# Two small softmax products with 64 stationary columns instead of twice 32

## The chip, the core and the metric

The kernel runs on one core of one Trainium2 chip. A core has a matrix engine (TensorE, PE in the profile; its weight loads are listed apart as PEld), VectorE (DVE), ScalarE (ACT) and GpSimd (POOL), and a SyncE (SP) that issues the DMA transfers here. The metric is the device time of one execution in microseconds, the median of the runs shown.

## The reference

A Fourier filter over the sequence, and then a mixture of experts with soft routing over all tokens of all batches:

```
X = np.fft.rfft(x, axis=1)                 # x: 8 batches, 2496 tokens, 256 channels
y = np.fft.irfft(X * (filt_r + 1j * filt_i), n=2496, axis=1)
x = y.reshape(8 * 2496, 256)
logits = x @ phi                           # 32 slots: 8 experts with 4 each
d = softmax of logits over the 19968 tokens    (dispatch)
slot_input = d.T @ x
slot_out = relu(slot_input @ w1[e]) @ w2[e]    (per expert, 256 -> 1024 -> 256)
c = softmax of logits over the 32 slots        (combine)
out = c @ slot_out
```

## The kernel before

The transform of 2496 points is split into 39 by 64. A first stage (`s1_unit`, L312 to L327, and `first_unit` for batch 0) multiplies by the 39-point matrix and puts the result through DRAM in another order; `x_unit` (L343) multiplies by the 64-point matrix C("b") and, on DVE and POOL, with the filter; `t_unit` (L369) transposes the filtered spectrum into the tiles `y`, and multiplies it by phi into the logits' spectrum `lts`. The inverse transform of the full 256 channels is never made: softmax needs only the logits in the token domain, which have 32 columns per batch, and the slot input is summed in the spectral domain.

The main loop (L734) has a slot for each pair of spectral columns, ten to a batch, and in each slot runs an x unit, the first-stage units that fall due, and a t unit two slots behind. When a pair of batches is through (GROUPS, four pairs), `chain(g)` (L409) is started for it, a generator that `hop` advances by one or more steps per slot, so that its work lies among the units. The last group's chain runs after the loop, with the held rest of the group before in its gaps (`behind`, L403), and then the experts (`h` at L859, `o` at L876) and the output products (L912).

A chain's steps, in order, with what the change and the prediction touch:

- `lsb` (L432 to L441): each batch's logits' spectrum, 5 tiles of 4 columns t by 32 slots, is transposed and copied by DVE.
- `v1` (L442 to L458): the inverse first stage. For each of the 20 columns t the spectrum (128 rows, 32 slots of one batch) is the stationary operand and one half of the constant `minv` (66 columns) the moving one. Two batches and two halves h give four products for a t. Each writes 32 partitions of one PSUM tile, so each sits in its own strip of 32 columns of the matrix engine. Seven t's fill a PSUM tile, which ACT copies into SBUF.
- `v`, `lg` (L459 to L486): transposes and the 39-point product give the logits `lg` in the token domain, with the running maximum (`cm`, `cmax`, `mt`, `mb`, `m_new`).
- `dispatch` (L512): DVE subtracts the maximum, ACT takes the exponential: `d`.
- `u` (L520 to L544): the forward first stage of `d`. For each of the 22 row blocks a (two halves h of 11) `d` for one batch (117 rows, 32 slots) is stationary and one half th of `w1d` (60 columns) moves: again four products with 32 partitions each.
- `u2`, `dd` (L545 to L571): transposes and the 64-point product give the spectrum of the dispatch weights.
- `z`, `s` (L573 to L613): with `dd` as the stationary operand, the sum of the weights and the slot input are accumulated over the `y` tiles. After its last use a `y` tile is free; the expert weights (`load_ws`, L725) are loaded into such tiles.
- the combine weights (L616 to L636): maximum, exponential and reciprocal sum over the slots. For groups 0 and 1 `lg` is put out to DRAM (L639) and read back for the tail (L785).

PE's work stands in the program order of the tile scheduler, which places instructions with a timeline of its own (L975). PE takes its instructions in order; only weight loads are pulled ahead. A matrix product in 32-bit floats is two records, and so is its weight load.

Of the kernel before, what the change touches and what calls it, by code (L numbers as in the profile page):

```python
# [9 lines left out]
F32 = mybir.dt.float32  # L10
F32R = mybir.dt.float32r
AF = mybir.ActivationFunctionType
ALU = mybir.AluOpType
# [6 lines left out]
NT = 20  # L20
NI = 22
NH = 11
PK = 3
KR = PK * N1
# [11 lines left out]
SLOTS = NE * SPE  # L36
GROUPS = ((0, 1), (2, 3), (4, 5), (6, 7))
NG = len(GROUPS)
NSPILL = 2
OUT_ORDER = (4, 5, 0, 1, 2, 3, 6, 7)  # L40
P = 128
SCALE = 2.0 / SEQ
NM = BATCH * SQ // P
KP = N2 + 2
# [162 lines left out]
def fft_soft_moe(ctx, tc, x, fr, fi, phi, w1, w2, cst, w1q, out):  # L207
    nc = tc.nc
    pe, dve, act, pool_e, sp = nc.tensor, nc.vector, nc.scalar, nc.gpsimd, nc.sync

    const = ctx.enter_context(tc.tile_pool(name="const", bufs=1))
    scr = ctx.enter_context(tc.tile_pool(name="scr", bufs=3, space=DRAM))
# [14 lines left out]
    r_all = const.tile([KR, NG, 4 * NH], F32, name="r_all")  # L227
# [6 lines left out]
    def C(name, lo=0, hi=None):  # L234
        o, rows, cols = OFF[name]
        hi = cols if hi is None else hi
        return cst_t[0:rows, o + lo : o + hi]
# [7 lines left out]
    lgp_cm, lgp = open_pool("lgp", 1, "left")  # L245
# [151 lines left out]
    c_dram = {}  # L397

    lgs = {}
# [9 lines left out]
    def chain(g):  # L409
        bs = GROUPS[g]  # L410
        wk = late_pool[0] if g == NG - 1 else work
# [4 lines left out]
        def copy(engine, dst, src):  # L416
            if g == NG - 1:
                engine = (dve, act)[flip[0] % 2]
                flip[0] += 1
            if engine is act:  # L420
                act.copy(dst, src)
            else:
                dve.tensor_copy(dst, src)
# [5 lines left out]

        nb = len(bs)  # L430
        R = nb * 64
        lsb = wk.tile([P, nb, NT, SLOTS], F32, tag="cc", name=f"lsb_{g}", bufs=1)  # L432
        for b2, b in enumerate(bs):
            lf = lsb[:, b2].rearrange("k t e -> k (t e)")
            for i0 in (0, 4):
                pl = psum([P, 4, P], f"ltr_{b}_{i0}")
                n = min(4, 5 - i0)
                for i in range(n):
                    pe.transpose(pl[:, i, :], lts[b][:, i0 + i, :], ident)
                copy(dve, lf[:, i0 * P : (i0 + n) * P], pl.rearrange("k i q -> k (i q)")[:, 0 : n * P])  # L440
            yield  # L441
        v1 = wk.tile([P, KP // 2, 2, NT], F32, tag="ca", name=f"v1_{g}", bufs=1)  # L442
        for t0 in range(0, NT, 7):
            n = min(7, NT - t0)
            pv = psum([P, 7, KP // 2, 2], f"v1_{g}_{t0}")
            for t in range(t0, t0 + n):
                for b2 in range(nb):
                    for h in range(2):
                        q = (b2 * 2 + h) * 32
                        pe.matmul(  # L450
                            pv[q : q + 32, t - t0].rearrange("q k r -> q (k r)"),
                            lsb[:, b2, t, :],
                            C("minv" if t else "minv0", h * KP, (h + 1) * KP),
                            start=True,
                            stop=True,
                        )
            copy(act, v1[0:R, :, :, t0 : t0 + n], pv[0:R, 0:n].rearrange("q t k r -> q k r t"))
            yield  # L458
        v = wk.tile([QP, NH, R], F32, tag="cb", name=f"v_{g}", bufs=1)  # L459
        lg_t = lgp.tile([KR, NH, nb, 2, SLOTS], F32, tag=f"lg{max(g, NSPILL)}", name=f"lg_{g}")  # L460
        lgs[g] = lg_t
        lg = lg_t.rearrange("s a b h e -> s a (b h e)")
        cm = wk.tile([KR, 3, SLOTS], F32, tag="cm", name=f"cm_{g}", bufs=1)
        v1f = v1.rearrange("q k r t -> q (k r t)")
        SA = 512 // R
        for s0 in range(0, NH, SA):
            n = min(SA, NH - s0)
            pv = psum([QP, SA, R], f"v_{g}_{s0}")
# [5 lines left out]
        for s0 in range(0, NH, SA):  # L474
            n = min(SA, NH - s0)
            pv = psum([KR, SA, R], f"lg_{g}_{s0}")
# [10 lines left out]
        nch = -(-NH // SA)  # L487

        NX = 2 * nb * NH
        lgf = lg_t.rearrange("s a b h e -> s (a b h) e")  # L490
        dve.tensor_reduce(out=cmax, in_=cm[:, 0:nch].rearrange("s c e -> s e c"), axis=AX.X, op=ALU.max)
        m_new, m_old = m_run[g], m_run[g - 1]
        pm = psum([SLOTS, KR], f"mt_{g}")
# [10 lines left out]
        else:  # L504
            dve.tensor_copy(m_new, pmb)
        d = wk.tile([KR, NX, SLOTS], F32, tag="cb", name=f"d_{g}", bufs=1)
        dv = d.rearrange("s (a b h) e -> s a b h e", b=nb, h=2)
        HT = NT // 2
        u = wk.tile([P, HT, 2 * N2], F32, tag="ca", name=f"u_{g}", bufs=1)
        mbc = m_new[0:KR].rearrange("s (o e) -> s o e", o=1)  # L510
# [9 lines left out]
        for a0 in range(0, NH, 4):  # L520
            n = min(4, NH - a0)
            if a0 + 4 < NH:
                dispatch(a0 + 4)
            pu = psum([P, 2, 4 * PK * 2, HT], f"u_{g}_{a0}")
            for h in range(2):
                for a in range(a0, a0 + n):
                    i = h * NH + a
                    kr, jn = (KR, PK) if i < NI - 1 else (N1, 1)
                    r0 = (a - a0) * 2 * PK
                    for b2 in range(nb):  # L530
                        for th in range(2):
                            q = (b2 * 2 + th) * 32
                            pe.matmul(
                                pu[q : q + 32, h, r0 : r0 + 2 * jn].rearrange("q r t -> q (r t)"),
                                dv[0:kr, a, b2, h, :],
                                C("w1d", th * PK * NT, th * PK * NT + jn * NT)[0:kr],
                                start=True,
                                stop=True,
                            )
            for h in range(2):  # L540
                k0 = (h * NH + a0) * PK * 2
                nk = min((h * NH + a0 + n) * PK, N2) * 2 - k0
                copy(act, u[0:R, :, k0 : k0 + nk], pu[0:R, h, 0:nk].rearrange("q r t -> q t r"))
            yield  # L544
        u2 = wk.tile([P, HT, nb, 2, SLOTS], F32, tag="cc", name=f"u2_{g}", bufs=1)  # L545
        for t0 in range(0, HT, SA):
            n = min(SA, HT - t0)
            pu = psum([P, SA, R], f"u2_{g}_{t0}")
            for t in range(n):
                pe.transpose(pu[:, t, :], u[0:R, t0 + t, :], ident[0:R, 0:R])  # L550
            copy(dve, u2[:, t0 : t0 + n].rearrange("k t b h e -> k t (b h e)"), pu[:, 0:n])
            if t0 != 0:
                yield
        dd = wk.tile([P, HT, nb, 2, SLOTS], F32, tag="cb", name=f"dd_{g}", bufs=1)
        for t0 in range(0, HT, SA):
            n = min(SA, HT - t0)
            pd = psum([P, SA, R], f"dd_{g}_{t0}")
            pe.matmul(
                pd[:, 0:n],
                C("b"),  # L560
                u2[:, t0 : t0 + n].rearrange("k t b h e -> k t (b h e)"),
                start=True,
                stop=True,
            )
            copy(act, dd[:, t0 : t0 + n].rearrange("k t b h e -> k t (b h e)"), pd[:, 0:n])
            if t0 == 0:
                dve.tensor_scalar(
                    out=dd[:, 0, :, 0, :], in0=dd[:, 0, :, 0, :], scalar1=C("wh"), scalar2=None, op0=ALU.mult
                )
            else:  # L570
                yield  # L571
# [4 lines left out]
        for b2 in range(nb):  # L576
            for j in range(4):
                pe.matmul(
                    pz[32 * j : 32 * j + 32, :], dd[:, 0, b2, 0, :], C("e0"), start=(b2 == 0), stop=(b2 == nb - 1)
                )  # L580
        if g > 0:
            al = wk.tile([P, SLOTS], F32, tag="al", name=f"al_{g}", bufs=1)
# [12 lines left out]
        for b2, b in enumerate(bs):  # L595
            for t in range(NT):
                j = t % 4
                with behind(g, b2 * NT + t):
                    pe.matmul(  # L599
                        pss[32 * j : 32 * j + 32, :],  # L600
                        dd[:, t % HT, b2, t // HT, :],
                        ys[b, t // 2][:, t % 2, :],
                        start=(b2 == 0 and t < 4),
                        stop=(b2 == nb - 1 and t >= NT - 4),
                    )
                if t % 8 == 7:
                    yield
# [27 lines left out]
        dve.tensor_scalar(out=rs, in0=rs, scalar1=1e-9, scalar2=None, op0=ALU.add)  # L635
        dve.reciprocal(out=rs, in_=rs)  # L636
        if g < NSPILL:
            c_dram[g] = scr.tile([KR, NH, nb, 2, SLOTS], F32, name=f"c_dram{g}", bufs=1)
            sp.dma_start(c_dram[g], lg_t)  # L639

    def load_tables(c):
# [139 lines left out]
    ltp_cm.__exit__(None, None, None)  # L781
    tail_cm, tail = open_pool("tail", 2, "left")
    for g in range(NSPILL):
        lgs[g] = tail.tile([KR, NH, len(GROUPS[g]), 2, SLOTS], F32, tag="cl", name=f"cl_{g}", bufs=NSPILL)
        sp.dma_start(lgs[g], c_dram[g])  # L785

    zr = const.tile([P, 1], F32, name="zr")
# [20 lines left out]
    def combine(pos):  # L808
# [4 lines left out]
        g, b2 = where[b]  # L813
        nb = len(GROUPS[g])
        cl = lgs[g]
        rv = r_all[:, g, 0 : 2 * nb * NH].rearrange("s (a b h) -> s a b h", b=nb, h=2)
        c1 = tail.tile([KR, 2, NH, SLOTS], F32, tag="c1", name=f"c1_{b}")
        for h in range(2):
            rb = rv[:, :, b2, h : h + 1].broadcast_to([KR, NH, SLOTS])
            nc.gpsimd.tensor_tensor(out=c1[:, h], in0=cl[:, :, b2, h], in1=rb, op=ALU.mult)  # L820
        cq = tail.tile([KR, 2, 4, SLOTS], F32, tag="cr", name=f"cr_{b}")
        nc.gpsimd.tensor_copy(cq[:, 0, 0:3], c1[:, 0, 8:11])
        nc.gpsimd.tensor_copy(cq[:, 0, 3:4], c1[:, 1, 8:9])
# [155 lines left out]
```

## Time and profile before

| | us |
|---|---|
| runs shown: median (lowest to highest) of 3 | 403.17 (401.98 to 403.49) |
| the profiled execution, its own time | 404.51 |
| its span, first to last instruction | 402.0 |
| mean granted TensorE clock | 0.955 |
| PE multiply records at L450 (v1), count and busy time | 640, 12.8 |
| PE multiply records at L533 (u), with 60 moving columns | 672, 10.9 |
| the same with 20 moving columns (the last block of 39 rows) | 32, 1.0 |

The profile lists each instruction with engine, line and times. "The chain of work that ended last" goes back from the last instruction to what released it, step by step; "issue" in it is time in which the engine waited for nothing that the profile shows. An entry of the chain is a start, a length and what ran. A window table gives for each stretch the busy time of every engine with the number of its instructions, then the granted clock, the share of the 16 DMA engines that was busy, and GB/s. Multiply records overlap in the engine, so a group's rate is read from its length in the chain or the timeline, not from the duration of one record.

### The profile page before, as it was taken

To read this page: it belongs to the slowest core of one execution; us is meant where nothing else is said; L and a number is where in the kernel's file an instruction comes from. 1 tells how busy PE (TensorE), PEld (TensorE's weight loads), DVE (VectorE), ACT (ScalarE), POOL (GpSimd) and SP (SyncE) were. 2 spreads that over 40 slices of the span, in tenths; PEclk is the share of its full clock that TensorE was granted. 3 is DMA by queue.
4 is the path that set the end of the run, shared out by engine and by line. 5 is a ranking of instruction groups with operands and counts; after the bars stand their busy time and mean duration, and the time that the engine had idled before them with its cause. 6 is when DMAs were issued, how large, how long until landed. Compare 5 with 4: busy or idle time off the path is not lost.

```text
span 402.0 us, 11841 instructions
## 1 busy us (share of the span) xinstructions
PE 354.6 (88%) x4769; PEld 285.2 (71%) x4769; DVE 263.0 (65%) x442; ACT 208.9 (52%) x412; POOL 209.7 (52%) x258
## 2 busy tenths in 40 slices
PE   7998989997999799999969998999767799899940
PEld 6996768885888587888857787887544544678830
DVE  2485829847679992977998474899225462477850
ACT  2765848775486654648676353435413131366630
POOL 0599969978377654947677364475700020244000
PEclk9999989999899899999999999999969899999975
DMA  8997899999489765967967464432857996399996
GB/s 267 371 296 221 255 332 332 358 338 325 134 239 298 233 188 159 302 213 228 338 211 234 113 187 146 133 108 76 296 207 259 329 288 255 132 386 414 414 415 283
DMA packets 53384, 103.65 MB, mean 258 GB/s; under 512 B 5375, under 2 KB 25983, under 8 KB 51027
## 3 DMA queue, kind: packets, MB, share of 16 engines
q1 hardware_dynamic: 53331, 102.92, 76.0%
q8 instruction: 37, 0.61, 0.6%
q14 instruction: 16, 0.13, 0.1%
HBM read 62.78 MB, written 40.12 MB: 256 GB/s over the span
## 4 chain that ended last, share of the span: by engine, by line
PE 72%; DVE 14%; issue 5%; DMA 3%; POOL 2%; ACT 1%; DVEq 0%; SPq 0%; ACTq 0%; POOLq 0%
PE x L350 15%; PE s L319 11%; PE t L375 8%; PE out L912 6%; PE s L599 4%; PE l L388 4%; PE s L276 3%; PE v L450 3%; PE lg L477 3%; DVE d L515 2%; DVE t L364 2%; DVE yt L363 2%; PE o L876 2%; PE h L859 2%; DMA xt<-in_x 2%
## 5 line engine op out<-in xcount | busy, mean ns | idle before, releaser
L309 POOL TENSOR_TENSOR xl<-xt,xh 117x512 fp32r<-117x512 f32 x77 | 105.1, 1373 | 28.5 <-ACT xh L308 24.6
L350 PE MATMUL x<-cst_t,ash 128*128 128x128 f32 x640 | 88.8, 281 | 7.1 <-issue 2.7
L350 PEld LDWEIGHTS x<-cst_t,ash 128*128 128x128 f32 x640 | 81.7, 196 | 12.9 <-issue 6.6
L367 POOL TENSOR_TENSOR yt<-yt,t 128x256 f32<-128x256 f32 x80 | 64.9, 812 | 32.1 <-DVE t L364 28.4
L363 DVE TENSOR_TENSOR yt<-x,fr_t 128x512 f32<-128x512 f32 x80 | 54.8, 684 | 35.4 <-PE x L350 19.6
L377 ACT COPY y<-t 128x512 f32<-128x512 f32 x80 | 46.9, 590 | 38.2 <-PE t L375 38.0
L308 ACT CAST xh<-xt 117x512 fp32r<-117x512 f32 x77 | 47.5, 623 | 24.6 <-PE s L319 14.4
L364 DVE TENSOR_TENSOR t<-x,fi_t 128x512 f32<-128x512 f32 x80 | 54.4, 680 | 3.2 <-POOL yt L367 3.2
L375 PE MATMUL t<-cst_t,yt 128*128 128x128 f32 x320 | 51.2, 280 | 3.0 <-DVE yt L366 2.6
L320 ACT COPY at<-s 120x512 f32<-120x512 f32 x77 | 44.9, 586 | 9.6 <-PE s L319 9.2
L375 PEld LDWEIGHTS t<-cst_t,yt 128*128 128x128 f32 x320 | 39.0, 144 | 13.5 <-issue 4.2
L366 DVE TENSOR_TENSOR yt<-yt,t 128x256 f32<-128x256 f32 x60 | 44.4, 751 | 0.8
L820 POOL TENSOR_TENSOR c<-cl,r_all 117x352 f32<-117x352 f32 x8 | 6.2, 798 | 62.2 <-PE ct L835 37.6
L319 PE MATMUL s<-xh,w1h 117*120 117x512 f32 x77 | 35.6, 463 | 1.5 <-ACT at L320 1.5
L319 PE MATMUL s<-xl,w1h 117*120 117x512 f32 x77 | 32.2, 418 | 0.1
L319 PE MATMUL s<-xh,w1l 117*120 117x512 f32 x77 | 31.5, 408 | 0.0
L912 PE MATMUL out<-so_h,st 32*128 32x256 f32 x312 | 27.7, 312 | 2.2 <-issue 1.3
L921 DVE COPY ob<-out 128x512 f32<-128x512 f32 (+1 forms) x40 | 24.9, 672 | 4.2 <-PE out L912 3.9
L921 ACT COPY ob<-out 128x512 f32<-128x512 f32 (+1 forms) x40 | 21.6, 578 | 11.0 <-PE out L912 9.3
L366 POOL TENSOR_TENSOR yt<-yt,t 128x256 f32<-128x256 f32 x20 | 15.6, 782 | 19.8 <-DVE t L364 17.4
L912 PE MATMUL out<-so_l,st 32*128 32x256 f32 x312 | 25.7, 291 | 0.0
L912 PEld LDWEIGHTS out<-so_h,st 32*128 32x128 f32 x312 | 20.5, 189 | 5.3 <-DVE ob L921 2.3
(112 smaller groups left out, 533.1 us busy)
## 6 DMA issues: line engine op xcount, KB each, us to landing
out<-ob SPq DMA_DIRECT2D x18, 1024.0 KB, 8.7
xt<-in_x SPq DMA_DIRECT2D x35, 512.0 KB, 5.9
ash<-a_dram SPq DMA_DIRECT2D x70, 256.0 KB, 4.9
a_dram<-at SPq DMA_DIRECT2D x70, 240.0 KB, 3.8
w<-in_w SPq DMA_DIRECT2D x64, 256.0 KB, 5.7
xt<-in_x SPq DMA_DIRECT2D x18, 256.0 KB, 4.9
c_dram<-lg SPq DMA_DIRECT2D x2, 643.5 KB
cl<-c_dram SPq DMA_DIRECT2D x2, 643.5 KB
```

The costliest lines, as they stand in the source:

```text
L308: act.copy(xh, xs)
L309: pool_e.tensor_tensor(out=xl, in0=xs, in1=xh.bitcast(F32), op=ALU.subtract)
L319: pe.matmul(ps, w, xx, start=(n == 0), stop=(n == 2))
L350: pe.matmul(ps[:, 2 * k + dh].rearrange("q r c -> q (r c)"), ash[:, k, dh * P : (dh + 1) * P], C("b"), start=True, stop=True,)
L363: dve.tensor_tensor(out=yt, in0=ps, in1=frv, op=ALU.mult)
L364: dve.tensor_tensor(out=t2, in0=ps[:, :, ::-1, :], in1=fiv, op=ALU.mult)
L366: add.tensor_tensor(out=yt[:, :, 1, :], in0=yt[:, :, 1, :], in1=t2[:, :, 1, :], op=ALU.add)
L367: pool_e.tensor_tensor(out=yt[:, :, 0, :], in0=yt[:, :, 0, :], in1=t2[:, :, 0, :], op=ALU.subtract)
L375: pe.transpose(pt[:, k, dh, :], yt[:, c % 2, 2 * k + dh].rearrange("q r c -> q (r c)"), ident)
L377: act.copy(y, pt.rearrange("k p h d -> k p (h d)"))
L912: last_mm[0] = nc.tensor.matmul(prs[k][:, mm, :], st[q, n % 2, c0 : c0 + P], (so_h, so_l)[n // 2][q, :], start=(n == 0), stop=(n == 3),).ins
L921: copied[k % 2] = copy(ob[:, nm * k : nm * (k + 1), :], prs[k]).ins
```

## The change

The two batches' slots are put side by side, so that one stationary tile holds 64 columns, 32 of each batch. v1 then has two products for a t and not four, u two for a block and not four; each writes 64 partitions. `lsb` changes its layout from (batch, t, slot) to (t, batch, slot), so DVE's copy into it writes runs of 32 elements with a step of 64. Everything behind takes the order (half, batch, slot) where it had (batch, half, slot): `lg`, `d`, `u2`, `dd`, the copies in DRAM and the combine weights. No sizes change there.

```diff
+        RH = nb * SLOTS
-        lsb = wk.tile([P, nb, NT, SLOTS], F32, tag="cc", name=f"lsb_{g}", bufs=1)
+        lsb = wk.tile([P, NT, nb, SLOTS], F32, tag="cc", name=f"lsb_{g}", bufs=1)
...
-                copy(dve, lf[:, i0 * P : (i0 + n) * P], pl.rearrange("k i q -> k (i q)")[:, 0 : n * P])
+                copy(
+                    dve,
+                    lsb[:, 4 * i0 : 4 * (i0 + n), b2, :],
+                    pl[:, 0:n].rearrange("k i (j e) -> k (i j) e", e=SLOTS),
+                )
...
             for t in range(t0, t0 + n):
-                for b2 in range(nb):
-                    for h in range(2):
-                        q = (b2 * 2 + h) * 32
-                        pe.matmul(
-                            pv[q : q + 32, t - t0].rearrange("q k r -> q (k r)"),
-                            lsb[:, b2, t, :],
-                            C("minv" if t else "minv0", h * KP, (h + 1) * KP),
+                for h in range(2):
+                    pe.matmul(
+                        pv[h * RH : (h + 1) * RH, t - t0].rearrange("q k r -> q (k r)"),
+                        lsb[:, t].rearrange("k b e -> k (b e)"),
+                        C("minv" if t else "minv0", h * KP, (h + 1) * KP),
...
-        lg_t = lgp.tile([KR, NH, nb, 2, SLOTS], F32, tag=f"lg{max(g, NSPILL)}", name=f"lg_{g}")
+        lg_t = lgp.tile([KR, NH, 2, nb, SLOTS], F32, tag=f"lg{max(g, NSPILL)}", name=f"lg_{g}")
...
-        dv = d.rearrange("s (a b h) e -> s a b h e", b=nb, h=2)
+        dv = d.rearrange("s (a h b) e -> s a h (b e)", b=nb, h=2)
...
-                    for b2 in range(nb):
-                        for th in range(2):
-                            q = (b2 * 2 + th) * 32
-                            pe.matmul(
-                                pu[q : q + 32, h, r0 : r0 + 2 * jn].rearrange("q r t -> q (r t)"),
-                                dv[0:kr, a, b2, h, :],
-                                C("w1d", th * PK * NT, th * PK * NT + jn * NT)[0:kr],
+                    for th in range(2):
+                        pe.matmul(
+                            pu[th * RH : (th + 1) * RH, h, r0 : r0 + 2 * jn].rearrange("q r t -> q (r t)"),
+                            dv[0:kr, a, h, :],
+                            C("w1d", th * PK * NT, th * PK * NT + jn * NT)[0:kr],
...
-        u2 = wk.tile([P, HT, nb, 2, SLOTS], F32, tag="cc", name=f"u2_{g}", bufs=1)
+        u2 = wk.tile([P, HT, 2, nb, SLOTS], F32, tag="cc", name=f"u2_{g}", bufs=1)
...
-        dd = wk.tile([P, HT, nb, 2, SLOTS], F32, tag="cb", name=f"dd_{g}", bufs=1)
+        dd = wk.tile([P, HT, 2, nb, SLOTS], F32, tag="cb", name=f"dd_{g}", bufs=1)
...
-                    out=dd[:, 0, :, 0, :], in0=dd[:, 0, :, 0, :], scalar1=C("wh"), scalar2=None, op0=ALU.mult
+                    out=dd[:, 0, 0], in0=dd[:, 0, 0], scalar1=C("wh"), scalar2=None, op0=ALU.mult
...
-                        dd[:, t % HT, b2, t // HT, :],
+                        dd[:, t % HT, t // HT, b2, :],
...
-            rb = rv[:, :, b2, h : h + 1].broadcast_to([KR, NH, SLOTS])
-            nc.gpsimd.tensor_tensor(out=c1[:, h], in0=cl[:, :, b2, h], in1=rb, op=ALU.mult)
+            rb = rv[:, :, h, b2 : b2 + 1].broadcast_to([KR, NH, SLOTS])
+            nc.gpsimd.tensor_tensor(out=c1[:, h], in0=cl[:, :, h, b2], in1=rb, op=ALU.mult)
```

More of the change, by code (lines that the diff above doesn't have):

```diff
@@ L431, in chain @@
         R = nb * 64
-        lsb = wk.tile([P, nb, NT, SLOTS], F32, tag="cc", name=f"lsb_{g}", bufs=1)
+        RH = nb * SLOTS
+        lsb = wk.tile([P, NT, nb, SLOTS], F32, tag="cc", name=f"lsb_{g}", bufs=1)
         for b2, b in enumerate(bs):
-            lf = lsb[:, b2].rearrange("k t e -> k (t e)")
             for i0 in (0, 4):
@@ L446, in chain @@
             for t in range(t0, t0 + n):
-                for b2 in range(nb):
-                    for h in range(2):
-                        q = (b2 * 2 + h) * 32
-                        pe.matmul(
-                            pv[q : q + 32, t - t0].rearrange("q k r -> q (k r)"),
-                            lsb[:, b2, t, :],
-                            C("minv" if t else "minv0", h * KP, (h + 1) * KP),
-                            start=True,
-                            stop=True,
-                        )
+                for h in range(2):
[3 more added lines that the diff above has]
+                        C("minv" if t else "minv0", h * KP, (h + 1) * KP),
+                        start=True,
+                        stop=True,
+                    )
             copy(act, v1[0:R, :, :, t0 : t0 + n], pv[0:R, 0:n].rearrange("q t k r -> q k r t"))
@@ L459, in chain @@
         v = wk.tile([QP, NH, R], F32, tag="cb", name=f"v_{g}", bufs=1)
-        lg_t = lgp.tile([KR, NH, nb, 2, SLOTS], F32, tag=f"lg{max(g, NSPILL)}", name=f"lg_{g}")
+        lg_t = lgp.tile([KR, NH, 2, nb, SLOTS], F32, tag=f"lg{max(g, NSPILL)}", name=f"lg_{g}")
         lgs[g] = lg_t
-        lg = lg_t.rearrange("s a b h e -> s a (b h e)")
+        lg = lg_t.rearrange("s a h b e -> s a (h b e)")
         cm = wk.tile([KR, 3, SLOTS], F32, tag="cm", name=f"cm_{g}", bufs=1)
@@ L489, in chain @@
         NX = 2 * nb * NH
-        lgf = lg_t.rearrange("s a b h e -> s (a b h) e")
+        lgf = lg_t.rearrange("s a h b e -> s (a h b) e")
         dve.tensor_reduce(out=cmax, in_=cm[:, 0:nch].rearrange("s c e -> s e c"), axis=AX.X, op=ALU.max)
@@ L529, in chain @@
                     r0 = (a - a0) * 2 * PK
-                    for b2 in range(nb):
-                        for th in range(2):
-                            q = (b2 * 2 + th) * 32
-                            pe.matmul(
-                                pu[q : q + 32, h, r0 : r0 + 2 * jn].rearrange("q r t -> q (r t)"),
-                                dv[0:kr, a, b2, h, :],
-                                C("w1d", th * PK * NT, th * PK * NT + jn * NT)[0:kr],
-                                start=True,
-                                stop=True,
-                            )
+                    for th in range(2):
[3 more added lines that the diff above has]
+                            C("w1d", th * PK * NT, th * PK * NT + jn * NT)[0:kr],
+                            start=True,
+                            stop=True,
+                        )
             for h in range(2):
@@ L550, in chain @@
                 pe.transpose(pu[:, t, :], u[0:R, t0 + t, :], ident[0:R, 0:R])
-            copy(dve, u2[:, t0 : t0 + n].rearrange("k t b h e -> k t (b h e)"), pu[:, 0:n])
+            copy(dve, u2[:, t0 : t0 + n].rearrange("k t h b e -> k t (h b e)"), pu[:, 0:n])
             if t0 != 0:
                 yield
-        dd = wk.tile([P, HT, nb, 2, SLOTS], F32, tag="cb", name=f"dd_{g}", bufs=1)
+        dd = wk.tile([P, HT, 2, nb, SLOTS], F32, tag="cb", name=f"dd_{g}", bufs=1)
         for t0 in range(0, HT, SA):
@@ L560, in chain @@
                 C("b"),
-                u2[:, t0 : t0 + n].rearrange("k t b h e -> k t (b h e)"),
+                u2[:, t0 : t0 + n].rearrange("k t h b e -> k t (h b e)"),
                 start=True,
@@ L564, in chain @@
             )
-            copy(act, dd[:, t0 : t0 + n].rearrange("k t b h e -> k t (b h e)"), pd[:, 0:n])
+            copy(act, dd[:, t0 : t0 + n].rearrange("k t h b e -> k t (h b e)"), pd[:, 0:n])
             if t0 == 0:
                 dve.tensor_scalar(
-                    out=dd[:, 0, :, 0, :], in0=dd[:, 0, :, 0, :], scalar1=C("wh"), scalar2=None, op0=ALU.mult
+                    out=dd[:, 0, 0], in0=dd[:, 0, 0], scalar1=C("wh"), scalar2=None, op0=ALU.mult
                 )
@@ L578, in chain @@
                 pe.matmul(
-                    pz[32 * j : 32 * j + 32, :], dd[:, 0, b2, 0, :], C("e0"), start=(b2 == 0), stop=(b2 == nb - 1)
+                    pz[32 * j : 32 * j + 32, :], dd[:, 0, 0, b2, :], C("e0"), start=(b2 == 0), stop=(b2 == nb - 1)
                 )
@@ L637, in chain @@
         if g < NSPILL:
-            c_dram[g] = scr.tile([KR, NH, nb, 2, SLOTS], F32, name=f"c_dram{g}", bufs=1)
+            c_dram[g] = scr.tile([KR, NH, 2, nb, SLOTS], F32, name=f"c_dram{g}", bufs=1)
             sp.dma_start(c_dram[g], lg_t)
@@ L783, in fft_soft_moe @@
     for g in range(NSPILL):
-        lgs[g] = tail.tile([KR, NH, len(GROUPS[g]), 2, SLOTS], F32, tag="cl", name=f"cl_{g}", bufs=NSPILL)
+        lgs[g] = tail.tile([KR, NH, 2, len(GROUPS[g]), SLOTS], F32, tag="cl", name=f"cl_{g}", bufs=NSPILL)
         sp.dma_start(lgs[g], c_dram[g])
@@ L815, in combine @@
         cl = lgs[g]
-        rv = r_all[:, g, 0 : 2 * nb * NH].rearrange("s (a b h) -> s a b h", b=nb, h=2)
+        rv = r_all[:, g, 0 : 2 * nb * NH].rearrange("s (a h b) -> s a h b", b=nb, h=2)
         c1 = tail.tile([KR, 2, NH, SLOTS], F32, tag="c1", name=f"c1_{b}")
         for h in range(2):
-            rb = rv[:, :, b2, h : h + 1].broadcast_to([KR, NH, SLOTS])
-            nc.gpsimd.tensor_tensor(out=c1[:, h], in0=cl[:, :, b2, h], in1=rb, op=ALU.mult)
+            rb = rv[:, :, h, b2 : b2 + 1].broadcast_to([KR, NH, SLOTS])
+            nc.gpsimd.tensor_tensor(out=c1[:, h], in0=cl[:, :, h, b2], in1=rb, op=ALU.mult)
         cq = tail.tile([KR, 2, 4, SLOTS], F32, tag="cr", name=f"cr_{b}")
```

## The prediction

> **What bounds the kernel now.** I read the page first, for the engines' shares and the DMA queues, then the chain of work that ended last in order of time, then the timeline and the window tables around the places where that chain shows idle time.
>
> ```profile
> PE 354.6 (88%) x4769; PEld 285.2 (71%) x4769; DVE 263.0 (65%) x442; ACT 208.9 (52%) x412; POOL 209.7 (52%) x258
> ...
> q8 instruction: 37, 0.61, 0.6%
> ...
> PE 72%; DVE 14%; issue 5%; DMA 3%; POOL 2%; ACT 1%; DVEq 0%; SPq 0%; ACTq 0%; POOLq 0%
> ```
>
> PE is the busiest engine and holds 72% of the chain. The next 5% is "issue", time in which PE waited for nothing that the profile shows. Here is where the chain has it, at the products that the change touches:
>
> ```profile
> 94.35 1.79 PE v L450 x111
> 97.22 2.12 issue
> 99.33 0.82 PE v L450 x18
> 100.56 1.71 PE x L350 x8
> 102.95 0.89 PE x L350 x8
> ...
> 242.53 1.33 issue
> ...
> 287.82 2.33 PE v L450 x136
> 290.15 3.89 issue
> 295.47 2.58 PE v L470 x11
> 298.04 3.71 PE lg L477 x6
> 301.75 1.86 PE s L599 x32
> ...
> 307.02 1.97 PE u L533 x141
> 308.98 3.89 issue
> 312.88 0.84 PE u L533 x35
> 314.45 2.40 PE u L550 x10
> 316.84 2.63 PE dd L558 x6
> ```
>
> Columns are start, length and what ran. The four gaps of 2.12, 1.33, 3.89 and 3.89 us, 11.2 us together, each stop PE in the middle of one run of equal products whose inputs are all there. The two long ones lie in the last chain, after the streaming loop, where nothing else feeds PE.
>
> What they are, the queue of instructions shows. The page has 37 packets and 0.61 MB on it, 16.5 KB each, for 2 x 4769 = 9538 PE records, so one packet per 258 records. The window 287.9 to 294.1, which ends with a gap, holds exactly one:
>
> ```profile
> q8 instruction: 1, 0.02, 1.1%
> ```
>
> A run of v takes 1.79 us for 112 multiply records and as many weight loads, 8 ns each; 258 such records are gone in 2.1 us. My reading: PE's program comes in blocks, the next is asked for when one is entered, and a dense run empties a block before the next has come. Whether a run has a gap then hangs on where the borders fall in it. That this is a fetch and not a hidden wait is an inference, and a rival below.
>
> After a gap PE also runs at half clock:
>
> ```profile
> 294.00:297.00 3.00, 2.19 (x21) 1.98 (x22) 0.57 (x1) 0.41 (x1) 0.00 (x0) 0.50 0.96 352
> 297.00:300.00 3.00, 3.00 (x8) 1.79 (x7) 0.91 (x2) 0.65 (x2) 0.00 (x0) 0.50 0.06 22
> ...
> 312.90:316.00 3.10, 2.32 (x43) 2.14 (x43) 0.75 (x2) 0.28 (x1) 0.00 (x0) 0.72 1.06 395
> ```
>
> The third number from the end is the granted clock: 0.50 for 6 us after the first long gap, 0.72 on the mean of the 3 us after the second.
>
> **The change part by part.** *Records.* v has 20 columns t, each now with two 64-wide products in place of four 32-wide; a product is two multiply records and two loads. Over four groups 640 multiply records become 320, u's 704 become 352: 672 multiply records and 672 loads fewer. A run of v shrinks from 320 records to 160 and u's from 352 to 176, both below the 258 of one block. So a border inside a run no longer leads to a second border within it: the four gaps should go, **-11.2 us**.
>
> *Clock.* Reference rows at full clock, from the chain at the first group:
>
> ```profile
> 104.78 0.88 PE v L470 x8
> ...
> 108.47 0.86 PE lg L477 x2
> ```
>
> And one from the timeline, for the next term:
>
> ```profile
> 128.36 1.89 PE L533 MATMUL u<-cst_t,d 117*32 117x60 f32 x128
> ```
>
> v's transposes: 11 at 0.11 is 1.21 against 2.58. lg: two of 0.86 and one of three quarters, 2.37 against 3.71. Together 2.7. u2 and dd have the same shapes: 10 transposes at 0.11 are 1.1 against 2.40, and dd's 2.5 x 0.86 = 2.15 against 2.63; 1.8, of which I take 1.2, as copies stand between. After the first gap x took 1.71 and not 0.89, so 0.8, with the t record beside it 1.0. Sum **-4.9 us**.
>
> *Pair against quartet.* Four v products go in 1.79 / 14 = 128 ns, four u products in 1.89 / 16 = 118 ns. No row has a 64-wide product, so it is bounded. A full-width product of 128 moving columns takes 0.89 / 4 = 222 ns, 1.74 ns a column: 115 ns for v's 66 columns, 104 ns for u's 60. Side by side a pair takes that, and the quartet, 13 and 14 ns above it, shows four at once. Lower end: 16 ns a record (1.79 us / 112) times four, 64 ns, if the quartet was held by records alone; over 80 v pairs and 88 u pairs -9.9 us. Upper end: one after the other, 230 and 208 ns, +16.1 us. I take 120 and 110, nearest to the quartet and the column rate, -1.3 us on PE; half is on the chain, **-0.6 us**.
>
> The Trainium skill, "TensorE: Matmul & The Clock Gate", section LDWEIGHTS, puts a load at its columns over 1.2 ns; four loads of 64 columns would be an estimated 213 ns per pair, the same as for the quartet's eight of 32. The quartet's measured 128 ns is below that, so loads into different column strips overlap; no run here shows it for two strips. By that rule the pair would be near the serial end, the third rival.
>
> *Copies.* lsb's copy now writes runs of 32 with gaps between.
>
> ```profile
> L423 DVE COPY lsb<-ltr 128x512 f32<-128x512 f32 x8 | 5.5, 683 | 8.5 <-PE ltr L439 8.5
> ```
>
> No row shows that pattern for DVE. As it must still read the same 512 columns from PSUM at 683 / 512 = 1.3 ns each, I take no change, and nothing makes it cheaper; the upper end, every write costing as much again, is 683 ns a copy, +5.5 us on DVE, of which the tail's two copies (+1.4 us) end a wait; the rest lies beside a busy PE. All other edits (d, u2, dd, lg, the spilled copies, the final weights c1) keep sizes and engines and swap two indices; DMA bytes are the same. The scheduler may place a few instructions otherwise, as its timeline sees shorter runs; I cost that at nothing, and its harm would be that of the first rival, data that comes late. A pair now needs both batches' lsb, but the second product of t=0 needed that before, so no wait is added; what queues behind it on PE is what queued before.
>
> *What is late next.* In the tail the expert weights.
>
> ```profile
> 305.46 9.84 SPq L722 DMA_DIRECT2D w<-in_w  x14
> 315.65 1.60 SPq L785 DMA_DIRECT2D cl<-c_dram  x2
> 320.20 14.99 SPq L722 DMA_DIRECT2D w<-in_w  x18
> ```
> ```profile
> 342.28 1.86 PE o L876 x26
> ```
> ```profile
> DMA to landing us min/median/max: 3.0/5.7/9.6
> ```
>
> The last load leaves at about 335 and lands near 340.5; its products end the run of 342.28 to 344.1, so about 3 us are spare. The 18 wait for y tiles that group 3's S products free, which move up by 11 to 12 us, but also stand behind the 14 and the two cl loads, with the DMA engines full (share 1.06 in the window from 312.9). That queue starts from group 2's S products at 301.75, which move up by one long gap and its clock, 3.9 + 2.7 = 6.6. The difference of 5 less the spare 3 is about **+1.5 us**. Another **+0.5** is for a shorter gap left at a border close to a run. In the streaming loop 2.1 + 1.3 + 1.0 = 4.4 us are won, where x units also wait for reloaded spectra and DVE is full at times; I let a quarter be lost, **+1.1**.
>
> Sum: -11.2 - 4.9 - 0.6 + 1.5 + 0.5 + 1.1 = -13.6 us. The output phase only starts earlier by what the tail wins. The profiled execution took 404.5 us (span 402.0 and 2.5 around it), so 390.9; the median of the three runs is 403.2, 1.3 below it, so the forecast is **389.6 us**.
>
> **The rivals.** *Data comes late instead.* The loop's 4.4 us are wholly absorbed and the weights, not group 3's S products, set the tail: 5 us in place of 1.5. Then -16.7 + 4.4 + 5 = -7.3, so **396**. For it: that DMA share. Against: the tail's DMA idles before the S products (share 0.06 at 297 to 300), which is room.
>
> *The gaps are not fetches.* The Trainium skill, "Runtime: NRT & Kernel Launch", section Instruction fetch mechanics, says that blocks of 256 instructions are fetched ahead and that the fetch hides behind an issue cost of some 20 cycles each. The trace's 8 ns a record speaks against that floor. As a mechanism of this kernel: a wait that no row shows holds PE after such runs, and stays when they shrink. Then only the pair's 0.6 us are won, **402.6**, no change.
>
> *The pair is serial* (the slower side). If two 64-wide strips do not run beside each other, or the load of one holds the other, v pairs take 230 and u pairs 208 ns, with 13 ns of switching as in the quartet 243 and 221: 80 x 115 + 88 x 103 = +18.3 us on PE. The gaps and the clock, -16.1, go just the same, and freed loop time is lost as above, +1.1: **406.5**. It decides from a pair of about 210 ns on. For it: no 64-wide product in the trace. Against: four strips side by side are shown.
>
> *Records alone held the quartet.* The pair takes 64 ns: half of 9.9 us more, **385**.
>
> **How the numbers follow.** Forecast 0.60 (386 to 393); data late 0.20; gaps not fetches 0.06; serial pair 0.07; records alone 0.07. The range is 384.5 to 397: it takes in the forecast, most of "records alone" and of "data late", and leaves the other two out. A measurement of this kernel tells 0.5% (2 us) from no change. Faster 0.60 + 0.20 + 0.07 = 0.87; the same 0.07, with the edge of "serial"; slower 0.06.
>
> **What would show it.** PE records fall by 672 and so do loads; the instruction queue has five packets fewer. In the chain no "issue" stands inside v L450 or u L533; a v run of 14 columns takes about 1.7 us. The granted clock stays at 1.0 behind the last v and u, and the S products of group 3 start 11 to 12 us earlier against the last lsb copy. A wait of o for w of 1 to 2 us appears. Wrong would be: gaps of the same length at the same places (not fetches), v runs of 3 us or more for 14 columns (serial), or x units idle for reloaded spectra by as much as the loop's gaps gave.

## The result and the profile after

The changed kernel takes 385.0 us (median of 4 runs, 384.03 to 386.2), the kernel before 403.33 us beside it (401.98 to 406.17): a ratio of 0.954, 95% interval 0.948 to 0.960. It is faster, inside the range on record, and 4.6 us below the forecast. The profiled execution took 384.03 us, its span is 382.1. Some executions of a kernel are slower as a whole than its others: the medians in this document include them, the ratios with their intervals do not.

The page of the changed kernel (engines, granted clock in 40 slices, queue of instructions, shares of the chain):

```profile
PE 347.8 (91%) x4097; PEld 278.3 (73%) x4097; DVE 268.4 (70%) x442; ACT 208.8 (55%) x412; POOL 213.9 (56%) x258
...
PEclk9999999999999999999999999999999999999975
...
q8 instruction: 32, 0.52, 0.5%
...
PE 63%; DVE 13%; DMA 11%; issue 3%; POOL 3%; ACT 2%; SPq 1%; DVEq 0%; ACTq 0%; POOLq 0%
```

PE lost 672 multiply records and 672 loads, the queue of instructions five packets, and the granted clock stays up until the last two slices. Its chain of waits in order of time (start, length, what ran), at the first run of v and in the tail:

```profile
92.59 1.81 PE v L452 x56
...
276.98 0.70 DVE lsb L423
277.73 2.60 PE v L452 x80
281.07 1.39 PE v L472 x11
282.46 2.53 PE lg L479 x6
...
290.26 2.85 PE u L533 x88
...
297.93 4.39 PE s L599 x80
...
313.41 1.86 PE o L876 x32
...
324.70 0.71 PE slot_out L885 x2
325.86 1.85 PE out L912 x41
```

No "issue" stands inside v or u any more: 80 records of v go through in 2.60 us and 88 of u in 2.85, each at full clock. The same marks in the chain of the kernel before, as far as the prediction does not show them:

```profile
287.08 0.70 DVE lsb L423
...
319.71 4.39 PE s L599 x80
...
335.19 1.86 PE o L876 x32
...
344.64 0.71 PE slot_out L885 x2
345.80 1.85 PE out L912 x36
```

From these rows the whole difference of the two spans can be laid out (us):

| stretch | before | after | difference | forecast |
|---|---|---|---|---|
| span's start to the first v | 94.35 | 92.59 | -1.8 | 0 |
| first v to the last lsb copy | 192.7 | 184.4 | -8.3 | -3.3 |
| last lsb copy to group 3's S products | 32.6 | 21.0 | -11.7 | -11 to -12 |
| S products to the first output product | 26.1 | 27.9 | +1.8 | +1.5 |
| first output product to the span's end | 56.2 | 56.2 | 0 | 0 |

The tail came as forecast. The streaming loop gave 5 us more than it should have. The first row holds no changed instruction: in profiles of kernels without added work the first v starts anywhere between 91.67 and 95.70 us, so its -1.8 is scatter of this one execution.

### The profile page after: what moved, and what is told of

It is laid out like the page before. It is cut to its first block, busy times and chain, and to the rows that moved or that the text cites. A ratio compares the mean times of both kernels' runs of the same rounds, so it can differ in the third digit from the quotient of the medians.

```text
span 382.1 us, 10497 instructions
## 1 busy us (share of the span) xinstructions
PE 347.8 (91%) x4097; PEld 278.3 (73%) x4097; DVE 268.4 (70%) x442; ACT 208.8 (55%) x412; POOL 213.9 (56%) x258
## 4 chain that ended last, share of the span: by engine, by line
PE 63%; DVE 13%; DMA 11%; issue 3%; POOL 3%; ACT 2%; SPq 1%; DVEq 0%; ACTq 0%; POOLq 0%
PE x L350 14%; PE s L319 10%; PE t L375 7%; DMA xt<-in_x 5%; PE out L912 5%; PE s L599 5%; PE l L388 3%; DMA out<-ob 3%; DVE t L364 3%; PE v L452 3%; PE lg L479 3%; PE o L876 2%; DVE yt L363 2%; DVE d L517 2%; PE h L859 2%
## 5 line engine op out<-in xcount | busy, mean ns | idle before, releaser
L350 PE MATMUL x<-cst_t,ash 128*128 128x128 f32 x640 | 86.4, 277 | 5.4 <-DMA ash<-a_dram 2.2
L350 PEld LDWEIGHTS x<-cst_t,ash 128*128 128x128 f32 x640 | 79.6, 191 | 11.9 <-issue 3.4
L367 POOL TENSOR_TENSOR yt<-yt,t 128x256 f32<-128x256 f32 x80 | 67.9, 849 | 20.0 <-DVE t L364 19.6
L364 DVE TENSOR_TENSOR t<-x,fi_t 128x512 f32<-128x512 f32 x80 | 54.2, 678 | 1.8 <-POOL yt L367 1.8
L366 DVE TENSOR_TENSOR yt<-yt,t 128x256 f32<-128x256 f32 x60 | 52.2, 880 | 0.8
L375 PE MATMUL t<-cst_t,yt 128*128 128x128 f32 x320 | 49.3, 276 | 2.0 <-POOL yt L367 1.5
L375 PEld LDWEIGHTS t<-cst_t,yt 128*128 128x128 f32 x320 | 37.7, 141 | 13.0 <-issue 5.4
L366 POOL TENSOR_TENSOR yt<-yt,t 128x256 f32<-128x256 f32 x20 | 15.6, 780 | 27.5 <-DVE t L364 21.2
L912 PE MATMUL out<-so_l,st 32*128 32x256 f32 x312 | 24.9, 284 | 0.0
```

What stands on the lines that cost most here:

```text
L350: pe.matmul(ps[:, 2 * k + dh].rearrange("q r c -> q (r c)"), ash[:, k, dh * P : (dh + 1) * P], C("b"), start=True, stop=True,)
L364: dve.tensor_tensor(out=t2, in0=ps[:, :, ::-1, :], in1=fiv, op=ALU.mult)
L366: add.tensor_tensor(out=yt[:, :, 1, :], in0=yt[:, :, 1, :], in1=t2[:, :, 1, :], op=ALU.add)
L367: pool_e.tensor_tensor(out=yt[:, :, 0, :], in0=yt[:, :, 0, :], in1=t2[:, :, 0, :], op=ALU.subtract)
L375: pe.transpose(pt[:, k, dh, :], yt[:, c % 2, 2 * k + dh].rearrange("q r c -> q (r c)"), ident)
L912: last_mm[0] = nc.tensor.matmul(prs[k][:, mm, :], st[q, n % 2, c0 : c0 + P], (so_h, so_l)[n // 2][q, :], start=(n == 0), stop=(n == 3),).ins
```

## The experiments

Times are medians, ratios are to the kernel before beside them. The kernel before took 403.3 us beside experiments 1 to 4, 405.3 beside 5, 6, 7 and 10, 409.0 beside 8 and 9 (401.84 to 414.05), and 405.4 beside 11.

**1 to 3. Parts of the change.** The new layout stays; u (experiment 1), v (2) or both (3) go back to four products of 32 columns. For u:

```diff
-                    for th in range(2):
-                        pe.matmul(pu[th * RH : (th + 1) * RH, h, ...], dv[0:kr, a, h, :], ...)
+                    for b2 in range(nb):
+                        for th in range(2):
+                            q = (th * nb + b2) * 32
+                            pe.matmul(pu[q : q + 32, h, ...], dv[0:kr, a, h, b2 * SLOTS : (b2 + 1) * SLOTS], ...)
```

> The new layout, v in pairs of 64 columns, u still in quartets of 32. Block theory (a gap opens where PE uses up a whole block of about 256 records before the next has come, so it belongs to the place of the block borders and not to a product): with 640 records fewer the borders fall elsewhere, and shifting the records of the trace of before accordingly leaves no 3.9 us gap in the last u run, although its quartets are unchanged; about 2 us of gap in all; 386 to 390 us. Rival (each run of quartets has its own hidden wait): u's last run keeps a gap of 3.9 us after some 140 records and its half clock of 1.2; 390 to 393 us.

> The new layout, u in pairs, v still in quartets. Block theory: the last v run keeps its gap (3.8 us), the first group's v too (2.1 us), the third group's v loses its gap and the second group's v, which had none, gets one of about 1.7 us; u has none; 394 to 398 us. Rival (own wait in each run): v's gaps stay at 2.1, none, 1.3 and 3.9 us in groups 0 to 3; 394 to 398 us as well, so the places decide and not the time.

> The new layout and order of slots, but v and u both in quartets of 32: as many records as before. Both theories: gaps of 2.1, 1.3, 3.9 and 3.9 us at the same places, 401 to 406 us. If the layout or the copies had a share in the gain, it is below 401.

Layout alone: 405.19 us, ratio 1.005 (0.9995 to 1.010), no gain. v alone: 389.44, ratio 0.971 (0.963 to 0.979). u alone: 399.78, ratio 0.995 (0.991 to 0.998). The chain of experiment 3 has the four gaps at their old places:

```profile
98.14 1.92 issue
...
243.04 1.60 issue
...
290.94 3.95 issue
...
309.70 4.34 issue
```

That of experiment 2, with v in quartets, has three, one of them in the second group's v, which ran through before:

```profile
97.48 1.70 issue
...
172.66 1.75 issue
...
292.50 3.20 issue
```

That of experiment 1 has only one in v or u, in the last run of u, which is in quartets there. It is the gap of about 2 us that the block theory gave, after 77 records of the run and not after 141 as before:

```profile
293.78 2.49 issue
```

The gap follows the dense run, and it moves to another group when the number of records ahead of that group changes, though nothing at that group was touched. The time of experiment 2 missed its 394 to 398: it kept 6.7 us of gaps and half clock behind them. The two parts alone won 13.9 and 3.5 us by the medians, 11.9 and 2.2 by the ratios.

**4. Useless records ahead of the program.** The kernel before, with the warm-up product cut to one column and 40 one-column products behind it, whose results nobody reads: 160 more records, so that all borders between blocks fall elsewhere, with PE's order behind them kept.

```diff
-        dve.memset(warm, 0.0)
+        dve.memset(warm[:, 0:32], 0.0)
...
-            pe.matmul(pw, warm[:, 0:P], warm, start=True, stop=True)
+            pe.matmul(pw[0:32, 0:1], warm[:, 0:32], warm[:, 0:1], start=True, stop=True)
+        for k in range(40):
+            q = 32 * (k % 4)
+            pe.matmul(pw[q : q + 32, 0:1], warm[:, 0:32], warm[:, 0:1], start=True, stop=True)
```

> The kernel before, with 160 more PE records that compute nothing: 40 products of 32 columns by 1 ahead of the first loads' arrival, which move every block border 160 records forward against the program. Block theory: the gaps of the last chain fall from 7.8 us to about 1 us, and the half clock behind them goes; in the loop the first and third group's v lose their gaps and the second group's v gets one of about 2.3 us; 390 to 395 us, faster by 8 to 13 us for useless work added. Rival (own wait in each run, or anything else tied to the products): all four gaps stay where they are, 403 to 405 us.

391.85 us, ratio 0.974 (0.969 to 0.979): 160 more records, and 11.5 us less time by the medians, 10.6 by the ratio, with v and u still in quartets. Its chain at the third group's u and in the tail:

```profile
267.10 1.26 issue
...
287.75 1.63 PE v L450 x92
...
299.31 2.52 PE u L533 x176
```

The last u runs through, the last v but for 0.25 us. Two details came otherwise than expected: the second group's v got no gap, and one of 1.26 us stands in the third group's u. So it is the place of a border in a run that makes a gap, and not a wait that belongs to v or u.

**5, 9, 10. The same records elsewhere.** Experiment 5 puts them into experiment 2, experiment 9 into the changed kernel, experiment 10 puts 128 instead of 160 into the kernel before.

> u in pairs, v in quartets as in the run with u alone, and the 160 idle records ahead of the program. Block theory: the gaps in v of groups 0, 1 and 3 (1.70, 1.75, 3.20 us) go with their half clock, the third group's v may get one of up to 2 us; 386 to 392 us. On the loop's extra gain: if u's pairs brought it by another placement of the transfers, the stretch from the second group's v to the third's is 66 to 68 us as in the changed kernel; if only the gaps count, it is 70 to 71 as in the kernel before.

> The kernel before with 128 idle records ahead of the program and the same order of every engine's work. Block theory, from shifting the borders through the trace of before: in the last chain a gap of about 1.6 us ahead of or early in v and one of 1.9 us early in u, in place of 3.9 and 3.9; none in v of groups 0 and 2, about 2.4 us in v of group 1; 393 to 398 us, between the kernel before and the run with 160. Rival (gaps belong to the products): 403 to 405 us with the gaps in place.

> The changed kernel (385.0 us) with 40 idle products, 160 PE records, ahead of the program, as they made the kernel before 11.5 us faster. Theory of the record blocks: in the changed kernel no run of pairs stops at any place of the border (a pair run holds 56 or 88 records, not 92 or 176), so there is no gap to take away: no gap over 0.6 us inside v or u, 384 to 388 us. Rival: the idle records help in another way (an engine that is warm, an earlier start): under 382 us here too.

Experiment 5: 389.92 us, ratio 0.963 (0.957 to 0.969), only 0.54 us of gap left in v. Its stretch from the second to the third v is 66.7 us, as in the changed kernel (66.2) and not as in the kernel before (70.6): with u in pairs this stretch gets shorter beyond the gaps, by what, experiment 11 shows. Experiment 10: 395.54, ratio 0.976 (0.969 to 0.983), inside its 393 to 398 though not to be told from experiment 4 by the ratio. Its gaps are where the theory put them, with other lengths in the tail: 2.34 us in the second group's v (2.4 expected), 1.01 in the last v (1.6) and 2.78 in the last u (1.9), none in v of the first and third group. Experiment 9: 385.2, ratio 0.953 (0.945 to 0.961), as the changed kernel without them, and no gap in its runs of v or u. Where the runs are in pairs, moving the borders wins nothing; that also excludes that the useless records help by themselves.

**6. The tail's weights.** In the changed kernel the two cl reads (L785) go behind the last weight load in SP's queue.

```diff
+            last_w[0] = sp.dma_start(t, w2[e, f])
...
+        with tc.issue_after(last_w[0].ins):
+            sp.dma_start(lgs[g], c_dram[g])
```

> The changed kernel, with the two reads of spilled logits put behind the last expert weight in SP's queue (nothing else moves). If the 1.8 us that the experts' second product waits for weights come from these two reads standing in front of the last 18 loads: the wait goes, 382.5 to 384 us. If the loads are late for another reason (the DMA engines full from earlier on): 384.5 to 386.

Its chain at the o products:

```profile
316.49 1.86 PE o L878 x32
...
325.95 0.71 PE slot_out L887 x2
```

o to slot_out takes 9.46 us here, 11.29 in the changed kernel and 9.45 before: the 1.8 us were the wait for w, behind cl in the queue. The time is 384.2 us, ratio 0.950 (0.946 to 0.954); 0.8 below the changed kernel, which these runs do not tell from no difference. It is the lowest median of all, and no version clearly beats the changed kernel.

**7 and 8. Two wrong ideas about the loop.** In the kernel before and in experiment 1, x and t wait in the second group, and the changed kernel waits less there. Experiment 7 puts the logits' spill behind the newest spectrum load in SP's queue, in case x waited for a transfer; experiment 8 makes VectorE reduce r_all behind x's newest product. Both are built on experiment 1.

```diff
+            with tc.issue_after(last_ash[0].ins):
+                sp.dma_start(c_dram[g], lg_t)
```
```diff
+            with tc.issue_after(last_t2[-1].ins) if g == 1 else nullcontext():
+                dve.tensor_reduce(out=rs[:, sl], in_=lgf[:, sl], axis=AX.X, op=ALU.add)
```

> v in pairs and u in quartets as in the first run, with the spill of the logits put behind the two reloads of spectra that stood behind it (SP's queue alone, two places each in groups 0 and 1). If the x units' waits of 1.0 and 1.6 us near 196 and 202 come from the reloads standing behind the spill: they shrink, the stretch from the second group's v to the third's goes from 71.2 to 68 to 70 us, 386.5 to 388.5 us in all. If they come from the reloads' own landing: 389 to 390.

> The kernel with v in pairs and u in quartets (389.4 us, stretch from the second to the third v 71.2 us), with one thing changed: in the second group VectorE reduces r_all only after the newest x unit's product t, as it happens to do with u in pairs. PE's order is the same. Theory: the stretch's extra 4 us over the changed kernel (66.2) come from VectorE's order, since x's products start when t ends: then the stretch falls to 68 to 69.5 us, the longest wait of x from 1.64 to under 0.9 us, the time to 386 to 388 us. Rival: that order follows from u's length and gives nothing by itself: stretch 71, time 389 to 390 us.

Experiment 7: 389.84 us, as experiment 1, and the waits did not shrink (1.03, 1.60 and 2.18 us; the stretch from the second to the third v grew to 73.9): it is not the spill ahead of the reloads. Nor is it the landing of a reload, which this run alone would leave open: in experiment 1's trace x starts at 203.38 after its long wait, and the reloads around it land at 195.95 and 206.75. Experiment 8: 391.0 us (387.4 to 392.27). The one wait fell, as its chain shows (experiment 1 has 1.62 us there),

```profile
202.01 0.83 issue
```

but the stretch from the second to the third v only from 71.2 to 70.5 us, just by that wait, and the time not at all. Both theories fell.

**11. The place of the first stage.** What was left was PE's own order. The group of x between the second and the third v, in the kernel before (count, busy time, mean ns, idle before):

```profile
L350 PE MATMUL x<-cst_t,ash 128*128 128x128 f32 x161 | 22.0, 277 | 2.7 <-issue 2.7
```

And in the changed kernel, which has 8 records fewer there:

```profile
L350 PE MATMUL x<-cst_t,ash 128*128 128x128 f32 x153 | 20.6, 277 | 0.2 <-DVE t L364 0.2
```

The stretches had not become shorter at equal work; work had moved between them. With u in pairs, in experiments 2 and 5 too, the scheduler puts first-stage products s ahead of u's last piece where it put them behind it with quartets. Experiment 11 is the changed kernel with that put back:

```diff
+                        u_last[g] = pe.matmul(
...
+            late_s = {(5, 1): 0, (7, 2): 1}.get((b, u))
+            with tc.issue_after(u_last[late_s].ins) if late_s is not None else nullcontext():
+                s1_unit(b, u)
```

> The changed kernel with only the place of the first stage put back: one first-stage unit of batch 5 stands behind the first group's last u product, one of batch 7 behind the second group's, where they stand with u in quartets (v and u stay in pairs). Counted by records, the stretch from the second to the third v held 161 x and 21 triples of the first stage before, and 153 and 19 in the changed kernel, whose x and t wait 3.0 us in the two stretches where they waited 6.3 us before. Theory: the scheduler's new placement of the first stage, which covers x's and t's waits with work, gave the loop its 3.3 us: then the stretch is back at 70 to 71 us with 161 x, the waits of x and t at 5.5 to 6.5 us, and the time 387.5 to 389.5 us. Rival: it is u's pairs themselves: waits of 3 us, stretch within 1 us of 66.2 by the work it holds, 385 us.

390.85 us (389.15 to 393.12), ratio 0.965 (0.960 to 0.970): 5.9 us above the changed kernel by the medians, 4.5 by the ratios, more than expected, with all v and u in pairs and the tail's v unchanged (2.60 us for 80). The stretch from the second to the third v is back at 70.9 us, with 161 x. What PE waited for between the first group's v and the third's, by the waits of the kernel before (in total, times, longest):

```profile
PE x L350 <- issue: 2.7, 2, 1.6
PE t L375 <- DVE yt L366: 2.6, 2, 1.6
PE x L350 <- PE x L350: 1.0, 1, 1.0
```

The same of the changed kernel:

```profile
PE x L350 <- PE x L350: 0.9, 1, 0.9
PE s L319 <- POOL xl L309: 0.8, 2, 0.5
PE x L350 <- PE t L375: 0.6, 1, 0.6
PE t L375 <- DVE yt L366: 0.5, 1, 0.5
...
```

And of experiment 11:

```profile
PE t L375 <- DVE yt L366: 3.2, 2, 1.6
PE x L350 <- issue: 1.0, 1, 1.0
PE x L350 <- PE x L350: 0.9, 1, 0.9
...
```

With two more of 0.2 us in each of the last two views, these are 6.3, 3.2 and 5.5 us. The new order gives PE first-stage products to do while DVE and POOL finish with x and t. The waits also cost clock. The window rows of experiment 11 behind its first two waits (the third number from the end is the granted clock):

```profile
130.00:134.00 4.00, 2.90 (x30) 2.45 (x31) 4.00 (x6) 1.64 (x5) 1.65 (x3) 0.62 0.65 171
134.00:137.00 3.00, 3.00 (x12) 2.57 (x11) 3.00 (x6) 2.01 (x5) 1.74 (x3) 0.50 0.90 316
137.00:140.00 3.00, 3.00 (x42) 2.51 (x43) 1.16 (x4) 0.00 (x0) 1.22 (x1) 0.87 0.73 214
```

Those of the changed kernel at the same step:

```profile
129.00:132.00 3.00, 2.35 (x35) 1.88 (x34) 3.00 (x5) 2.53 (x7) 0.65 (x2) 1.00 0.76 215
132.00:136.00 4.00, 4.00 (x47) 3.39 (x49) 3.95 (x9) 1.62 (x3) 3.99 (x5) 1.00 0.97 348
```

4 x 0.38 + 3 x 0.50 + 3 x 0.13 = 3.4 us of clock lost in the first, none in the second. With the 5.5 - 3.2 = 2.3 us of waits that is 5.7. Its chain has the first and the last v at

```profile
94.94 1.80 PE v L453 x56
...
286.15 2.60 PE v L453 x80
```

so 191.2 us lie between them, and 277.73 - 92.59 = 185.1 in the changed kernel, 6.1 less. PE's order in experiment 11 is not that of experiment 1 in every other place, so a part of the 6.1 may come from those places.

## Why the prediction was right, and where it was off

**Records and gaps: right.** The counts fell as worked out, and all four gaps went, 11.2 us. That they were fetches of the next block was called an inference. Experiments 2 and 4 bear it out: gaps move and vanish with the number of records ahead of them, where a wait of v or u on data would have stayed.

The traces of the instruction queue show it directly. In the kernel before, the gap in the last v stands from 290.15 to 294.04 us, and a packet starts at 291.58 and ends at 292.63, 1.4 us before PE goes on. The 13 profiles show 25 gaps of 0.5 us or more as "issue" in v, u or the output products; in each of them a packet ends 1.3 to 1.6 us before PE goes on, while the packets of the kernel before come some 11 us apart (37 in 402 us). One of these gaps, 1.29 us at 384.76 in the output products of the kernel before, was not counted in the prediction; the output takes 56.2 us with and without it.

2 x 4097 records in 32 packets are 256 each. The Trainium skill, "Runtime: NRT & Kernel Launch", section Instruction fetch mechanics, gives the same 256 to a block, which the trace confirms, and holds that the fetch is hidden, which experiment 4 contradicts by some 11 us. That a run of pairs is shorter than a block need not be the whole cure: a pair's 8 records go in 129 ns, 16 ns a record, so a block also lasts twice as long as with quartets. Nor are pairs wholly free of gaps: the last u of experiment 11 stops for 0.54 us. The +0.5 us that the sum held for such a gap was not needed in the profile of the changed kernel.

**Clock: right in the tail, too small in the loop.** The tail's v transposes take 1.39 us for 11 and lg 2.53 for 6, where 1.21 and 2.37 were reckoned from 2.58 and 3.71. In the loop I counted 1.0 us for the half clock behind the first gap and overlooked a second place. Window rows of the kernel before:

```profile
135.00:141.00 6.00, 5.96 (x99) 4.80 (x100) 6.00 (x12) 2.03 (x5) 2.04 (x3) 0.72 0.82 282
...
99.00:103.00 4.00, 3.67 (x33) 3.48 (x33) 0.70 (x2) 1.00 (x3) 0.06 (x1) 0.57 0.29 112
```

That is 6 x 0.28 = 1.7 and 4 x 0.43 = 1.7 us lost in the kernel before; the one at 135 follows waits of x and t, not a gap.

**Pair against quartet: the right mechanism, a wrong size.** Two strips run side by side, so the serial rival fell; but they do not reach the column rate. A pair of v takes 1.81 / 14 = 129 ns and one of u, over all 22 blocks, 2.85 / 22 = 130 ns, where I took 120 and 110. The quartets take 128 in v, and 2.52 / 22 = 115 over the same blocks of u (experiment 4), so that is 80 x 1 + 88 x 15 = +1.4 us on PE and not -1.3: of the whole gain nothing comes from the products themselves.

**Copies: right.** A copy into lsb takes 681 ns, 683 before, and experiment 3 has the new layout and no gain or loss.

**Late weights: right.** +1.8 us against 1.5 (the terms given, 5 less 3, make 2), at the o products, whose weight loads wait 1.9 us for w where they waited 0.2 before, by the queue that I named; experiment 6 takes it away by moving cl.

**The loop: the step that failed.** "The scheduler may place a few instructions otherwise, as its timeline sees shorter runs; I cost that at nothing, and its harm would be that of the first rival". It did place them otherwise, and on the other side: not data that comes late but waits that are covered, 3.2 us between the first and the third v in place of 6.3. Putting the first-stage units back cost 5.9 us by the medians and 4.5 by the ratios (experiment 11). How much it is worth hangs on the clock: 3.4 of the 6.1 us in experiment 11's profile are half clock, which does not always follow such waits. Experiment 1 has the old placement too and full clock in its loop; from the first v to the last lsb copy it takes 186.9 us, 2.5 more than the changed kernel, though its u in quartets takes 1.0 us less there.

With that step goes the +1.1 us that I let be lost of the loop's gain. The loop's -8.3 us is made up of gaps -3.4, waits 3.2 - 6.3 = -3.1, clock -3.4, and pairs 60 x 1 + 66 x 15 = +1.0, in all -8.9; 0.6 us stay unaccounted for. With the old placement, experiment 11 stands at 390.85 us, 1.3 from the forecast of 389.6. The mechanisms that the sum reckoned with were there, but so close a match is in part chance: the pair, the +0.5 and the +1.1 were each off, and experiment 11 has its own half clock.

**The rivals.** Gaps that are not fetches, a serial pair and records alone are excluded by the rows above. The measured 385.0 us is the very number that "records alone" gave, 0.5 us inside the lower end of the range, but a pair takes 129 ns and not its 64: that the range reached so far down was luck, not foresight. Late data happened in the tail with the size of the forecast, and not in the loop.

What stays open: why the scheduler chose the new order. Experiments 2 and 5 show that it goes with u in pairs and experiment 1 that it does not go with v in pairs; how its timeline came to it was not looked into. Nor does the placement explain the whole loop: experiment 5 has it, with full clock and 0.54 us of gap, and takes 188.3 us from the first v to the last lsb copy, 3.9 more than the changed kernel, 2.8 of them behind the third v; with v in quartets the order there is another, and what it costs was not tested.

## What to carry to other kernels

A gap in the middle of a run of equal products whose inputs are all there, shown as "issue", is to be compared with the packets of the instruction queue: a run of some 8 ns a record empties a block of 256 before the next one has come. Such a gap is tested cheaply by a few idle records ahead of the program, and cured by fewer records in the dense run; beyond that, a change in the number of records anywhere ahead can move the time by several us (11 in experiment 4), and looks like an effect of what was changed. Before two stretches between marks are compared, count the records in them, since a scheduler that sees shorter products moves work across the marks.

## What the hardware showed beside that

Useless records made the kernel before faster by 10.6 us by the ratio, 11.5 by the medians (experiment 4), and left the changed one as it was (experiment 9).

A pair of 64-column products takes 129 ns with 66 moving columns and 126 to 129 with 60 (64 records of u in 2.01 us in experiment 9 and 2.06 in experiment 2), while the quartets take 128 and 118. At the 1.74 ns a column of the full-width product, 6 columns would make 10 ns, so something other than the column rate holds the pair. What that is, no run here shows.

A wait of 1.61 us behind one of 0.89 brought half clock in experiment 11, and one of 1.61 behind 0.97 in the kernel before; 0.89, 0.47 and 0.65 in the changed kernel did not. But 1.61 behind 1.03 in experiment 1 left the clock at full, and so did 1.60 behind 0.96 in experiment 4, so the length of the waits alone does not decide it. Of the eight profiles with the old placement, whose waits at this step are 0.9 to 1.0 and 1.6 us, six have half clock behind them for 3.4 or 6.8 us; of the five with the new placement none has.

Waits of x that the profile puts down as "issue" were waits for DVE where it was looked at; experiment 8, which put DVE's product earlier, halved one of them. In experiment 1's timeline x starts 0.1 us after DVE's product t (L364) has read the bank before it:

```profile
202.61 0.67 DVE L364 TENSOR_TENSOR t<-x,fi_t 128x512 f32<-128x512 f32 x1
...
203.38 1.13 PE L350 MATMUL x<-cst_t,ash 128*128 128x128 f32 x8 [1.64 <-issue]
```
